# Cosformer attention and a gated FFN on one core: q and k of batch 4 loaded before batch 3's q is turned, and three tiles staged elsewhere

## The chip, the cores and the metric

One core of one Trainium2 chip runs the whole kernel. The time is device microseconds of one execution, as the median of some runs. One execution was also profiled; all times of single instructions come from that one.

## What is computed

```python
# q, k, v: (8 batches, 8 heads, 576 rows, 64); phi doubles 64 to 128 columns
phi(x) = concat(relu(x) * cos_row, relu(x) * sin_row)
kv  = phi(k)^T @ [v, 1]                        # per batch and head, 128 x 65
x   = (phi(q) @ kv)[:, :64] / (phi(q) @ kv)[:, 64]   # numerators / denominator
x   = x as (4608 tokens, 512)
out = (gelu(x @ w_gate) * (x @ w_val)) @ w_out        # 512 -> 1536 -> 512
```

Inputs and outputs are fp32 in HBM; the matmuls run in bf16.

## The kernel before, in words

The 4608 tokens are cut into eight batches of 576 for the attention and nine blocks of 512 for the FFN, so a batch's rows spill over block borders: block 2 takes the last 128 tokens of batch 1 and the first 384 of batch 2 (tiles t = 0, 1, 2 of 128 rows), block 3 takes t = 3 and 4 of batch 2 and the first 320 of batch 3. While TensorE (PE) works on the FFN of block n, the attention of batch n + 1 is made between its steps. The order of every engine's instructions is that of the Python text: nothing is reordered by a scheduler, and each engine runs its own list from front to back and waits where its next instruction must wait. SyncE (SP) is such a list too: it issues nearly all loads, stores and turns.

One batch goes through these stages:

- `load` (L95) brings q, k or v into a staging place. `stage` (L84) says which: st has three slots of 128 x 2304 fp32; sm and fs are two more places that later hold sums (sm the halves of hidden activations and partial products, L504; fs the differences of x).
- `prep` (L169) and `prep_both` (L183) scale: relu times sine on ACT, relu times cosine on ACT or DVE, into the tile phis. `prep_both` does q and k of a batch in one instruction of 128 x 512. `cast_v` (L207) casts half of v to bf16 (vx).
- `turn_q` (L220) writes qT, phi(q) transposed, by two DMA transposes. There is one qT; a new turn must wait until the numerators of the batch before have read it.
- `kv_unit` (L264) makes kv on PE in banks 6 and 7, ACT copies it.
- `nm_unit` (L309) makes the numerators of one tile t: 8 matmuls into two banks (6 and 7 unless told otherwise), then three DVE instructions (L322 to L324) that divide and leave x_sb. The next use of the banks waits for them.
- `turn_x` (L375) transposes x_sb by DMA into xT of the blocks concerned.

The FFN of a block has 12 steps jt, each 128 hidden columns: `gv_unit` (L420) makes 4 matmuls for gate and 4 for value, ACT the Gelu (L439), DVE the product (L442). It takes banks 0 and 1 or 2 and 3 in turn. In blocks 1 and 2 the first steps are cut into two halves of 256 tokens, because the later half of the block's x comes later: two units a step. `o_step` (L938) adds one or two of the seven half-size products that make the output matmul of the block before (L547, Strassen's scheme); sums come from DVE (L529), and ACT or DVE copies some partial products to sm (L565), in block 2 ACT. From block 3 on the gate and value matmuls use the same scheme (`group`, L650), with four differences of x made by POOL (`x_sum`, L630), and an ACT copy (L669) between the first two and the third of its products.

Around the change: `block1` (L975) is the FFN of block 1 with the attention of batch 2 and the scaling of q(3) and k(3) (batch in brackets); `block2` (L1025) is that of block 2 with the attention of batch 3 and the scaling of batch 4. Which loads SP issues at the end of which step stands in the table LOADS (L899), keyed by block and step; "0, 5" is the first five of nine row groups j of all heads, and a single 0 or 2 the first or second half of the heads. EARLY (L1015) says in which step of block 2 which row group of batch 4 is scaled, s for sine and c for cosine. SCALE (L964) does that for k(2), q(3) and k(3); keys from 12 on are steps of block 2.

SP's list between the turn of q(2) and block 3 is: turn q(2); load k(3); turn x(1,4); at steps 9 to 11 turn x(2,0), half of v(3), turn x(2,1), half of v(3), turn x(2,2); in block 2 turn q(3), turns x(2,3) and x(2,4), loads of batch 4 in six pieces, stores and the turns of x(3,t).

Of the kernel before, what the change touches and what calls it, by code (L numbers as in the profile page):

```python
# [16 lines left out]
def kernel(  # L17
# [13 lines left out]
    nc = tc.nc  # L31
# [8 lines left out]
    R = S // 64  # L40
# [25 lines left out]
    def bank(i):  # L66
        return ps[:, i]
# [13 lines left out]
    sm = sums.tile([128, NP * R * D], FP32)  # L81
    fs = fast.tile([128, 6 * BLK], FP32)

    def stage(name, b):  # L84
        early = {
            ("q", 1): 1, ("k", 1): sm, ("v", 1): fs, ("k", 2): 2, ("v", 2): 1,
            ("q", 3): fs, ("k", 3): 0, ("v", 3): 2,
            ("q", 5): 1, ("k", 5): 0, ("q", 7): 1, ("k", 7): 0,
        }
        at = early.get((name, b), "qkv".index(name))  # L90
        if isinstance(at, int):
            return st[:, at]
        return at[:, 0:NP * R * D].rearrange("p (m x) -> p m x", m=NP)
# [65 lines left out]
    act_copy, dve_copy = nc.scalar.copy, nc.vector.tensor_copy  # L159
# [5 lines left out]
    def phi_tile(name, b):  # L165
        phi[name, b] = phis[:, 1 if name == "k" else 2 * (b % 2) * (b > 2)]
        return phi[name, b]
# [15 lines left out]
    def prep_both(b, part, j, eng):  # L183
        for name in "qk":
            phi_tile(name, b)
        o = phis[:, b % 2:b % 2 + 2, :, j, part * D:(part + 1) * D]
        o = o.rearrange("p a m d -> p (a m) d")
        i = st[:, 0:2, :, j * D:(j + 1) * D].rearrange("p a m d -> p (a m) d")
        tab = (cos_t, sin_t)[part]
        if eng is nc.scalar:  # L190
            nc.scalar.activation(o, i, AF.Relu, scale=tab[:, j:j + 1])  # L191
        else:
            eng.tensor_scalar(o, i, 0.0, tab[:, j:j + 1], op0=ALU.max, op1=ALU.mult)
# [13 lines left out]
    def cast_v(b, m0, m1, copy, j0=0, j1=R):  # L207
        copy(  # L208
            vx[:, m0:m1, j0:j1, 0:D],
            staged["v", b][:, m0:m1, j0 * D:j1 * D].rearrange("p m (j d) -> p m j d", d=D),  # L210
        )
# [15 lines left out]
    def q_cols(b, t, h):  # L227
        c0 = min(t * 128, S - 128)
        return qT[b][:, h % 2, h // 2, c0:c0 + 128]
# [79 lines left out]
    def nm_unit(b, t, b0=6):  # L309
        for h in range(H):  # L310
            nc.tensor.matmul(  # L311
                bank(b0 + h // 4)[:, (h % 4) * (D + 1):(h % 4 + 1) * (D + 1)],
                lhsT=q_cols(b, t, h),
                rhs=kv_sb[b][:, h // 2, h % 2, :],
                start=True,
                stop=True,
            )
        nm = ps[:, b0:b0 + 2, 0:4 * (D + 1)].rearrange("p g (h d) -> p g h d", h=4)
        den = attn2.tile([128, 2, 4], FP32, name="den")
        rec = attn2.tile([128, 2, 4], FP32, name="rec")  # L320
        x = xsp.tile([128, 2, 4, D], BF16, name="x_sb")
        nc.vector.tensor_scalar_add(den, nm[:, :, :, D], EPS)  # L322
        nc.vector.reciprocal(rec, den)
        nc.vector.tensor_tensor(  # L324
            x,
            nm[:, :, :, 0:D],
            rec[:, :, :, None].to_broadcast([128, 2, 4, D]),
            op=ALU.mult,
        )
        xs[b, t] = x.rearrange("p g h d -> p (g h d)")  # L330
# [30 lines left out]
    def xT_block(blk):  # L361
        if blk not in xT:
            xT[blk] = xtp.tile([128, CT, BLK], BF16, name="xT")
        return xT[blk]

    def pieces(b, t):

        o = max(128 * (t + 1) - S, 0)
        c0, n = b * S + t * 128, 128 - o
        while n > 0:  # L370
            m = min(n, BLK - c0 % BLK)
            yield c0 // BLK, c0 % BLK, o, m
            c0, o, n = c0 + m, o + m, n - m

    def turn_x(b, t):  # L375
        x = xs.pop((b, t))
        for blk, c, o, m in pieces(b, t):
            nc.sync.dma_start_transpose(
                out=xT_block(blk)[:, :, c:c + m], in_=x[o:o + m, :]
            )  # L380

    def turn_x_pe(b, t, to, copy):
        x = xs.pop((b, t))
        p = bank16(to)[:, 0:CT * 128].rearrange("p (c n) -> p c n", c=CT)
        for ct in range(CT):
            nc.tensor.transpose(
                out=p[:, ct, :], in_=x[:, ct * 128:(ct + 1) * 128], identity=ident
            )
        for blk, c, o, m in pieces(b, t):
            copy(xT_block(blk)[:, :, c:c + m], p[:, :, o:o + m])  # L390
# [64 lines left out]
    def flush(engs=(nc.sync, nc.sync)):  # L455
        for i, o_sb in stores:
            store(engs, i, o_sb)
        stores.clear()
# [437 lines left out]
    def js(a, b):  # L896
        return tuple(range(a, b))

    LOADS = {  # L899
        (1, 2): [(3, "k")], (1, 9): [(3, "v", 0)], (1, 10): [(3, "v", 2)],  # L900
        (2, 2): [(4, "q", 0, 5), (4, "k", 0, 5), (4, "q", 5, R), (4, "k", 5, R), (4, "v")],
        (2, 9): [(5, "q", 0, 5), (5, "k", 0, 5)],
        (3, 1): [(5, "q", 5, R), (5, "k", 5, R), (5, "v")],
        (3, 9): [(6, "q", 0, 5), (6, "k", 0, 5)],
# [53 lines left out]
    def scale(b, name, sines_, cosines):  # L958
        for j in sines_:
            prep(name, b, 1, (j,), eng=nc.scalar)  # L960
        for j in cosines:
            prep(name, b, 0, (j,))
# [12 lines left out]
    def block1():  # L975
        b, n = 2, 1
        for jt in range(JT):
            i = jt - 9
            if i > 0:
                nm_unit(b, i, (6, 4, 6)[i])  # L980
                turn_x(b, i)
            if jt < 2:
                for i in range(2):
                    half, unit = divmod(2 * jt + i, 2)
                    x3 = lambda: turn_x_pe(1, 3, 5, dve_copy)
                    gv_unit(n, unit, half * HALF, HALF, between=x3 if jt == i == 0 else None)
                    j = JA + 2 * jt + i
                    prep("q", b, 1, (j,), eng=nc.scalar)
                    prep("q", b, 0, (j,))
            else:  # L990
                gv_unit(n, jt, between=(lambda: nm_unit(b, 0, 6)) if i == 0 else None)
            if i == 0:
                turn_x(b, 0)
            if jt % 3 == 1:
                flush()
            if jt == 2:
                prep("q", b, 0, (R - 1,))
                prep("q", b, 1, (R - 1,), eng=nc.scalar)
                turn_q(b)
                nm_unit(1, NT - 1)  # L1000
            if jt == 3:
                turn_x(1, NT - 1)
            if jt == 6:
                kv_unit(b)
            if jt in SCALE:
                scale(*SCALE[jt])
            if jt in (3, 4):
                cast_v(b, 2 * (jt - 3), 2 * (jt - 3) + 2, act_copy)
            if jt == 11:
                nm_unit(b, 3, 4)  # L1010
            start_loads(n, jt)
            if 4 <= jt < 8:
                wo_sum(("T3", "T1", "T2", "T4")[jt - 4])

    EARLY = {  # L1015
        5: "s0 c0", 6: "s1 c1 s2", 7: "c2 s3 c3", 8: "s4 c4", 9: "s5 c5", 10: "s6 c6",
        11: "s7 c7", 12: "s8 c8",
    }

    def early(jt):  # L1020
        for what in EARLY.get(jt, "").split():
            part = "cs".index(what[0])
            prep_both(4, part, int(what[1]), nc.scalar if part or jt > 7 else nc.vector)

    def block2():  # L1025
        b, n = 3, 2
        for jt in range(JT):
            if jt >= 4:
                gv_unit(n, jt, to=(2, 6) if jt == JT - 1 else None)
            else:  # L1030
                for i in range(2):
                    half, unit = divmod(2 * jt + i, 4)
                    gv_unit(n, unit, half * HALF, HALF)
                    if jt == i == 0:
                        nm_unit(2, 4)
                        turn_q(3)
            if 0 <= jt - 6 < NT:
                turn_x(b, jt - 6)
            if jt < JT - 1:
                o_step(n, jt)  # L1040
            if 0 <= jt - 5 < NT:
                nm_unit(b, jt - 5)
            if jt + JT in SCALE:
                scale(*SCALE[jt + JT])
            if jt < 2:
                cast_v(b, 2 * jt, 2 * jt + 2, act_copy)
            if jt == 3:
                kv_unit(b)
            early(jt)
            if jt == 1:  # L1050
                turn_x(2, 3)
                turn_x(2, 4)
            start_loads(n, jt)
            if jt in (8, 9):
                m = 2 * (jt - 8)
                cast_v(4, m, m + 2, (act_copy, dve_copy)[jt - 8])
            more(n, jt)

    turn[0] = 1
    block1()  # L1060
    block2()

    PREPS = {
# [124 lines left out]
```

## Time and profile before

| what | us |
|---|---|
| median of 3 runs | 313.39 (312.26 to 313.79) |
| the profiled execution | 313.79 |
| its span, first to last instruction | 311.4 |
| PE busy | 298.2 (96%) |
| DVE, ACT, POOL busy | 228.7, 201.4, 153.4 |
| PE clock, mean granted | 0.991 |

How to read it. The page cuts the span into 40 slices and gives each engine's busy share in tenths. A timeline row is: start, duration, engine, line of the kernel, operation, what it writes <- what it reads, shape, how many in a row, and in brackets how long the engine idled before it and what ended that. A q behind an engine's name is its issuing of DMAs. Of a DMA the profile also has the time from its issue to its landing. A wait list gives who waited, for whom, the total, how often and the longest.

In the profiled execution step 11 of block 1 ends on PE at 78.44 us, block 2 runs from 79.26 to 118.01 and block 3 begins there. The pieces of batch 4 that SP issued in block 2:

| load | issued at | us to landing |
|---|---|---|
| q, j 0 to 4 (640 KB) | 94.68 | 6.0 |
| k, j 0 to 4 (640 KB) | 95.31 | 7.0 |
| q, j 5 to 8 (512 KB) | 95.86 | 8.0 |
| k, j 5 to 8 (512 KB) | 96.35 | 9.0 |
| v, first half (576 KB) | 97.17 | 9.6 |
| v, second half (576 KB) | 97.98 | 10.3 |

### The profile page before, as it was taken

The page shows a single profiled execution, that of the slowest core. Times are in us where ns is not written, and L with a number is a line of the kernel's source. Part 1 is how long each engine was busy: PE and PEld are TensorE (multiplying, and loading weights), DVE is VectorE, ACT ScalarE, POOL GpSimd, SP SyncE. Part 2 cuts the span into 40 slices and gives each one's busy share as a digit, 9 for nine tenths or more (in the row PEclk, how much of TensorE's full clock was granted, in tenths as well). Part 3 has the DMA queues.
Part 4 walks back from the last instruction along what each step waited for, and adds up shares of the span by engine and source line. Part 5 has one row for each costly group of instructions (what it writes and reads, how often), then busy time and mean ns, then how long its engine had stood idle before and what let it go on. Part 6 is the DMA issues. An engine that isn't in the chain of part 4 may idle for free.

```text
span 311.4 us, 7900 instructions
## 1 busy us (share of the span) xinstructions
PE 298.2 (96%) x3071; PEld 225.9 (73%) x3071; DVE 228.7 (73%) x495; ACT 201.4 (65%) x394; POOL 153.4 (49%) x130
## 2 busy tenths in 40 slices
PE   8799999999899599999999999999999999999993
PEld 3574456655686267788878877878898888888882
DVE  5856996899973764788678867885779785866772
ACT  7864684997471578878587858785556465565530
POOL 6675430000000056737773777379965867297420
PEclk9999999999999989999999999999999999999998
DMA  7999999989997957996899699966652421213035
GB/s 277 246 178 239 319 308 396 301 119 217 199 157 233 293 122 204 124 353 129 222 121 360 129 216 122 344 103 108 93 107 40 93 42 37 45 24 69 1 78 126
DMA packets 73172, 53.66 MB, mean 172 GB/s; under 512 B 45392, under 2 KB 62544, under 8 KB 73136
## 3 DMA queue, kind: packets, MB, share of 16 engines
q1 hardware_dynamic: 63360, 41.17, 58.8%
q0 software_dynamic: 9696, 11.93, 16.7%
q8 instruction: 24, 0.39, 0.5%
q14 instruction: 12, 0.10, 0.1%
q10 hardware_dynamic: 80, 0.07, 0.1%
HBM read 37.75 MB, written 9.44 MB: 152 GB/s over the span
## 4 chain that ended last, share of the span: by engine, by line
PE 75%; DMA 7%; DVE 6%; issue 6%; ACT 3%; POOL 1%; SPq 1%; POOLq 0%; ACTq 0%; DVEq 0%
PE ps L650 29%; PE ps L547 19%; PE ps L430 17%; PE ps L463 3%; PE ps L311 3%; DMA st<-in_v_dram 2%; DMA st<-in_k_dram 2%; PE ps L270 2%; DMA wv_sb<-in_moe_w_val_dram 2%; DVE hT L442 2%; ACT phis L177 1%; DVE phis L179 1%; ACT vx L208 1%; POOL st L529 1%; ACT gel L439 1%
## 5 line engine op out<-in xcount | busy, mean ns | idle before, releaser
L630 POOL TENSOR_TENSOR fs<-xT 128x512 bf16<-128x512 bf16 x12 | 13.9, 1158 | 74.9 <-DVE den L322 66.8
L529 POOL TENSOR_TENSOR sm<-hT 128x768 bf16<-128x768 bf16 x24 | 39.4, 1641 | 20.1 <-PE ps L650 13.3
L430 PE MATMUL ps<-xT,wv_sb 128*128 128x512 bf16 (+1 forms) x208 | 49.1, 359 | 0.0
L430 PE MATMUL ps<-xT,wg_sb 128*128 128x512 bf16 (+1 forms) x208 | 48.3, 355 | 0.6 <-ACT phis L177 0.4
L442 DVE TENSOR_TENSOR hT<-gel,ps 128x512 bf16<-128x512 f32 (+1 forms) x52 | 32.1, 623 | 15.6 <-PE ps L430 11.2
L650 PE MATMUL ps<-fs,ws 128*128 128x256 bf16 x288 | 41.7, 273 | 0.0
L650 PEld LDWEIGHTS <-ws 128*128 128x128 bf16 x384 | 36.2, 98 | 4.6 <-ACT ps L669 0.3
L547 PEld LDWEIGHTS <-sm 128*128 128x128 bf16 x336 | 33.2, 99 | 6.5 <-issue 0.5
L439 ACT ACTIVATE gel<-ps 128x512 f32<-128x512 f32 (+1 forms) x52 | 28.3, 548 | 14.6 <-PE ps L430 13.4
L682 ACT ACTIVATE gel<-ps 128x512 f32<-128x512 f32 x30 | 17.9, 597 | 30.0 <-PE ps L650 30.0
L650 PE MATMUL ps<-xT,wg_sb 128*128 128x256 bf16 x240 | 36.0, 273 | 0.0
L690 DVE TENSOR_TENSOR ps<-fs,ps 128x512 f32<-128x512 f32 x30 | 20.9, 695 | 20.4 <-PE ps L650 14.2
L547 PEld LDWEIGHTS <-hT 128*128 128x128 bf16 x288 | 28.2, 98 | 6.2 <-issue 1.0
L430 PEld LDWEIGHTS <-wv_sb 128*128 128x128 bf16 x208 | 20.3, 98 | 17.0 <-issue 0.5
L560 DVE TENSOR_TENSOR o_sb<-sm,ps 128x256 f32<-128x256 f32 x56 | 23.4, 419 | 9.0 <-ACT sm L565 7.0
L191 ACT ACTIVATE phis<-st,sin_t 128x512 bf16<-128x512 f32 x36 | 25.7, 717 | 5.7 <-DMA st<-in_k_dram 5.7
L430 PEld LDWEIGHTS <-wg_sb 128*128 128x128 bf16 x208 | 19.3, 98 | 13.9 <-DMA xT<-x_sb 0.5
L529 POOL TENSOR_TENSOR sm<-hT,sm 128x768 bf16<-128x768 bf16 x12 | 19.7, 1642 | 15.7 <-PE ps L547 13.1
L324 DVE TENSOR_TENSOR x_sb<-ps,rec 128x512 bf16<-128x512 f32 x38 | 26.3, 691 | 1.3
L650 PEld LDWEIGHTS <-wg_sb 128*128 128x128 bf16 x240 | 23.1, 98 | 5.4
L177 ACT ACTIVATE phis<-st,sin_t 128x256 bf16<-128x256 f32 (+1 forms) x57 | 23.9, 480 | 1.5 <-DMA st<-in_k_dram 1.5
L547 PE MATMUL ps<-wo_sb,hT 128*128 128x256 bf16 x192 | 23.7, 272 | 0.9 <-DVE x_sb L324 0.9
(126 smaller groups left out, 590.5 us busy)
## 6 DMA issues: line engine op xcount, KB each, us to landing
out_dram<-o_sb SPq DMA_DIRECT2D x69, 128.0 KB, 3.0
st<-in_v_dram SPq DMA_DIRECT2D x12, 576.0 KB, 7.4
st<-in_q_dram SPq DMA_DIRECT2D x5, 640.0 KB, 5.0
st<-in_q_dram SPq DMA_DIRECT2D x5, 512.0 KB, 4.5
st<-in_k_dram SPq DMA_DIRECT2D x4, 640.0 KB, 6.0
st<-in_k_dram SPq DMA_DIRECT2D x4, 576.0 KB, 4.8
st<-in_q_dram POOLq DMA_DIRECT2D x4, 576.0 KB, 12.4
st<-in_k_dram SPq DMA_DIRECT2D x4, 512.0 KB, 5.3
```

The source lines that it names most:

```text
L177: nc.scalar.activation(o, i, AF.Relu, scale=tab[:, j:j + 1])
L191: nc.scalar.activation(o, i, AF.Relu, scale=tab[:, j:j + 1])
L324: nc.vector.tensor_tensor(x, nm[:, :, :, 0:D], rec[:, :, :, None].to_broadcast([128, 2, 4, D]), op=ALU.mult,)
L430: nc.tensor.matmul(bank(to[g])[:, 0:w], lhsT=wt[:, ct, js], rhs=xt[:, ct, c0:c0 + w], start=(ct == 0), stop=(ct == CT - 1),)
L439: nc.scalar.activation(gel[:, 0:w], bank(to[0])[:, 0:w], AF.Gelu)
L442: nc.vector.tensor_mul(hT[n][:, jt, c0:c0 + w], gel[:, 0:w], bank(to[1])[:, 0:w])
L529: eng.tensor_tensor(a[name][:, j0:j1], a[x][:, j0:j1], a[y][:, j0:j1], op=op)
L547: nc.tensor.matmul(at, lhsT=hs.setdefault(key, h_parts(n, p))[a][:, j], rhs=ts[b][:, j], start=(j == 0 and i in ((1, 2, 4, 5), (1, 4, 5))[ ...
L560: nc.vector.tensor_tensor(o, got[key, k], x, op=op)
L650: nc.tensor.matmul(to[:, 256 * half:256 * half + 256], lhsT=w_part(a, j * 128, (j + 1) * 128)[:, ct], rhs=xb[self.n][b][:, ct], start=(hal ...
L682: nc.scalar.activation(self.gel0, self.other, AF.Gelu)
L690: nc.vector.tensor_tensor(bank(val), self.m5, self.sum, op=ALU.add)
```

## The change

k(3) is staged in slot 2 instead of 0 and v(3) in sm instead of slot 2, which leaves slots 0 and 1 empty in block 1. k(3) and the first half of v(3) are loaded at step 4 of block 1 (k(3) stood at step 2, ahead of the turn of x(1,4)), the second half of v(3) at step 9, and the first halves of q(4) and k(4) at the end of step 11, ahead of the turn of q(3); they stood behind it. The numerators of batch 2's t = 3 go from step 11 of block 1 (banks 4 and 5) to behind the first unit of block 2 (banks 6 and 7), and those of t = 4 from there to behind the first unit of step 1, with the turn of q(3) behind them. The casts of v(3) come a step earlier, and so do those of v(4), which are now both on ACT. The scaling of batch 4 begins at step 4 and has one row group a step.

```diff
     early = {
         ("q", 1): 1, ("k", 1): sm, ("v", 1): fs, ("k", 2): 2, ("v", 2): 1,
-        ("q", 3): fs, ("k", 3): 0, ("v", 3): 2,
+        ("q", 3): fs, ("k", 3): 2, ("v", 3): sm,
...
     LOADS = {
-        (1, 2): [(3, "k")], (1, 9): [(3, "v", 0)], (1, 10): [(3, "v", 2)],
-        (2, 2): [(4, "q", 0, 5), (4, "k", 0, 5), (4, "q", 5, R), (4, "k", 5, R), (4, "v")],
+        (1, 4): [(3, "k"), (3, "v", 0)], (1, 9): [(3, "v", 2)],
+        (1, 11): [(4, "q", 0, 5), (4, "k", 0, 5)],
+        (2, 2): [(4, "q", 5, R), (4, "k", 5, R), (4, "v")],
...
             if jt == 11:
-                nm_unit(b, 3, 4)
+                cast_v(3, 0, 2, act_copy)
             start_loads(n, jt)
...
     EARLY = {
-        5: "s0 c0", 6: "s1 c1 s2", 7: "c2 s3 c3", 8: "s4 c4", 9: "s5 c5", 10: "s6 c6",
+        4: "s0 c0", 5: "s1 c1", 6: "s2 c2", 7: "s3 c3", 8: "s4 c4", 9: "s5 c5", 10: "s6 c6",
         11: "s7 c7", 12: "s8 c8",
     }
...
-            prep_both(4, part, int(what[1]), nc.scalar if part or jt > 7 else nc.vector)
+            prep_both(4, part, int(what[1]), nc.scalar if part or jt > 8 else nc.vector)
...
                     gv_unit(n, unit, half * HALF, HALF)
-                    if jt == i == 0:
-                        nm_unit(2, 4)
+                    if i == 0 and jt < 2:
+                        nm_unit(2, 3 + jt)
+                    if i == 0 and jt == 1:
                         turn_q(3)
             if 0 <= jt - 6 < NT:
                 turn_x(b, jt - 6)
+            if jt == 0:
+                cast_v(b, 2, 4, act_copy)
             if jt < JT - 1:
                 o_step(n, jt)
...
-            if jt < 2:
-                cast_v(b, 2 * jt, 2 * jt + 2, act_copy)
...
             start_loads(n, jt)
-            if jt in (8, 9):
-                m = 2 * (jt - 8)
-                cast_v(4, m, m + 2, (act_copy, dve_copy)[jt - 8])
+            if jt in (7, 8):
+                m = 2 * (jt - 7)
+                cast_v(4, m, m + 2, act_copy)
             more(n, jt)
```

## The prediction

> **What bounds the kernel now.** I read the page's slices first, then TensorE's waits between 80 and 180 us, then the timeline around the longest wait, then SyncE's own row of issues.
>
> ```profile
> PE   8799999999899599999999999999999999999993
> PEclk9999999999999989999999999999999999999998
> ```
>
> A slice is 7.8 us. PE is full except in the first slices, the 5 (101 to 109 us) and the end, so only time that PE loses counts. The 8 of PEclk stands just after the 5.
>
> ```profile
> PE ps L311 <- DVE x_sb L324: 3.1, 1, 3.1
> PE ps L547 <- DVE x_sb L324: 0.9, 1, 0.9
> ```
>
> These are nearly all of PE's waits in that window; both lie in block 2. The timeline shows what stands behind the long one:
>
> ```profile
> 95.31 0.45 SPq L98 DMA_DIRECT2D st<-in_k_dram  x1
> ...
> 102.44 0.72 ACT L191 ACTIVATE phis<-st,sin_t 128x512 bf16<-128x512 f32 x1 [5.67 <-DMA st<-in_k_dram]
> 102.46 0.49 DVE L193 TENSOR_SCALAR phis<-st,cos_t 128x512 bf16<-128x512 f32 x1 [3.29 <-DMA st<-in_k_dram]
> 103.07 0.58 ACT L439 ACTIVATE gel<-ps 128x512 f32<-128x512 f32 x1
> ...
> 103.68 0.69 DVE L442 TENSOR_TENSOR hT<-gel,ps 128x512 bf16<-128x512 f32 x1 [0.73 <-ACT gel L439]
> ...
> 105.98 0.69 DVE L324 TENSOR_TENSOR x_sb<-ps,rec 128x512 bf16<-128x512 f32 x1
> ...
> 106.72 0.42 PE L311 MATMUL ps<-kv_sb,qT 128*128 128x65 bf16 x8 [3.13 <-DVE x_sb L324]
> ```
>
> To be read upwards: PE waits for the evacuation of the numerators before (same two banks); that stands in DVE's queue behind a unit's product, which waits for ACT's Gelu; and both engines sat in front of batch 4's scaling until the first half of its k landed, 7.0 us after its issue. SyncE tells why that issue came at 95.31:
>
> ```profile
> 81.59 8.78 SPq L222 DMA_TRANSPOSE qT<-phis  x2
> 90.47 4.11 SPq L378 DMA_TRANSPOSE xT<-x_sb  x2
> 94.68 0.52 SPq L98 DMA_DIRECT2D st<-in_q_dram  x1
> ```
>
> The turn of batch 3's q and two turns of x hold SyncE for 13.1 us before the load.
>
> **Price of the long wait.** 3.13 us idle, and a slow clock after it: the windows view has 0.50 from 108 to 111 us. In the chain of waits the next eight matmuls of L430 take 2.56 us instead of 1.73, six of L547 1.28 instead of 0.66, eight of L311 0.44 instead of 0.26: 0.83 + 0.62 + 0.18 = 1.6. Together **4.7 us**. Behind it PE shows no wait over 0.2 us, so I let a gain here reach the end whole.
>
> **The loads ahead of the turn.** After the change SyncE reaches q and k of batch 4 behind the turn of x(2,2), which issues at 80.30 and takes 1.2: 81.5. Their slots are free (q of batch 2 scaled by 63 us, v of batch 2 cast by 67.5). With the 6.0 and 7.0 us to landing of today's issues they are there by about 89, and the first scaling comes at step 4, about 94.5. The wait is gone: **4.7 won**. Two 640 KB issues of 0.5 us each are only moved.
>
> **What is late next: the turn of q(3).** It rewrites qT, which the numerators of t=4 read, and these now stand behind unit 2 of step 1. I follow PE there. Its unit of step 11 ends at 78.44; the first unit of block 2 needs the turn of x(2,0). Today that issues at 75.72 and lands 3.4 later (79.1) behind both halves of k(3), issued at 70.45 and 71.84. Now the turn of x(1,4) goes first (1.2 us), k(3) at 71.65 (landing 5.0 later and 1.4 after that: 76.6, 78.0), half of v(3) behind it (1.45, as between the two halves of v(4): 79.5), and only then x(2,0). Bounds: 79.1 if half of v costs nothing, 80.5 if all is in turn; I take 79.8. PE: first unit 79.9, unit 0.87, numerators 0.26, unit 0.87: 81.9, where the pair of products starts; today 82.48, after the 0.86 us wait for banks 4 and 5, which goes because the numerators now use 6 and 7. Of those 0.6 us 0.26 is given back when t=4's numerators come; a 0.19 wait at 86.35 may go too. **0.4 won**, bounds -0.3 and 1.1.
>
> Then products 1.31, unit 0.87, numerators 0.26: the turn of q(3) issues at 84.4, not 81.59: 2.8 later. The two turns took 6.5 and 7.8 us to landing, 13.0 from the first issue to the second landing, with x(2,2) ahead of them until 86.1. Elsewhere (121.42 to 132.15) it is 10.7. So qT is complete between 95.1 and 97.4; its first reader, the numerators of t=0 at step 5, is at 97.50 today and at 97.1 then. Cost 0 to 0.3; I take 0.1.
>
> One page speaks against this order: the Trainium skill, "DMA: Bandwidth & Descriptors", section "Queues, rings and completion order", says that each DMA engine consumes a ring's descriptors in order. By it the 1.28 MB put ahead delay the turn; k's half would land near 87.5, and with the 8.6 us between the landings at 86.1 and 94.6 qT would be complete at 96.1, inside the range above.
>
> **v(4) on ACT.** The remaining four loads follow the turns. SyncE's way from turn to load was 13.1 us, with x turns of 2.0; with the 1.2 of the other x turns and 8.8 for the pair it is 11.2. So the first load goes at 95.6 to 97.5. A first load lands 4.5 (at 113.93) to 6.0 later (at 94.68), each further one 1.5 behind: half of v(4) is there 7.5 to 9.0 after the first issue, 103.1 to 106.5; middle 104.8. Today its cast runs at 112.53 at step 8; now at step 7, where ACT arrives at about 102.6. So ACT waits 0.5 to 3.9 us there, **a new wait**, and behind it stand the Gelu of step 8, the copies to sm, the scaling. How long may it? From the cast's start the next rows are spaced 1.04 (cast), 0.49 (Gelu), 0.25 (copy), 0.62 (sine), 0.61 (cosine). Up to block 3's first copy there are 2 casts, 4 Gelus, 2 copies, 4 sines, 3 cosines, and 0.58: 9.4 us. Without a stall PE needs that copy at 119.71 - 4.7 - 0.4 = 114.6, so the cast may start at 105.2. The numerators of t=4 of batch 3 (PE at 108.3) need the evacuation before them: cast and Gelu 1.65, unit's product 0.6, den to x_sb 1.1: 3.4 after the cast's start, so **104.9**. The middle value fits; the late end costs 1.6. I count 0.
>
> **The rest.** k(3) lands 1.1 later (78.0 for 76.9), but DVE first reads it at 78.62; ACT loses 1.1 there, where it idled 0.71 and 0.94 just after and DVE reached the unit's product only at 82.34. The casts of v(3) (1.14 each) move into ACT's 2.38 us of idle before 83.96; v's second half, issued at 77 without the wait for its slot, lands by 82 as before. Were that cover gone, ACT's copy to sm would slip by a cast, 1.1 us. One cast goes from DVE (0.85) to ACT; it is in the 9.4. The scaling of batch 4 begins a step earlier, 0.72 on ACT and 0.48 on DVE a step, where both idle over 1.2 us a step today (1.78 and 1.36 before step 5's Gelu and product). The subtractions on POOL (from 111.79) need the turn of x(3,2), which comes earlier with its evacuation; block 3 reads the first of four.
>
> **Sum.** 4.7 + 0.4 - 0.1 = 5.0. The profiled execution took 313.79 (span 311.4 and 2.4 around it), the slowest of three, 0.4 over their median 313.39. 313.79 - 5.0 = **308.8**; from the median it would be 308.4, and I keep the first.
>
> **Rivals.**
> 1. *The cast of v(4) is the new stall.* For it: the half lands at 106.5 at the late end, today it needs 9.6 us from its own issue, and it was moved a step earlier. Against: two loads fewer stand ahead. PE loses 1.6, up to 2.5 if the turn is late too: 310.4 to 311.3.
> 2. *Block 2 starts late.* If x(2,0) lands at 81 or later behind k and v of batch 3, PE idles 2.7 us instead of 1.4; 0.4 won becomes 0.9 lost: 310.1. Against: 1.7 MB were never that slow (1.45 us per 576 KB).
> 3. *Slower: the preload holds up the turn of q(3).* If its 3.2 us (two loads at 1.6) come on top of the slowest turn, qT is complete at 100.6, and PE waits 3.5 at t=0's numerators; after 3.1 the clock fell, so 1.6 more; the loads behind go at 100.7 and v comes at 109.7, 1.3 after the then allowed 108.4. 6.4 lost against 5.1 won: 315.1. It decides from a landing of qT of about 100. Against: the loads are issued 2.9 us before the turn, while PE still works towards it.
> 4. *The preload isn't early*, because SyncE waits at its slot or because scaling waits for the second halves: the 4.7 stay: 313.4.
>
> **Chances.** Forecast 0.52; rival 1 0.22; rival 2 0.09; rival 3 0.10; rival 4 0.07. The range takes the forecast, rivals 1 and 2: below it 0.7 more at the start of block 2 and 0.7 for the runs (half of their spread of 1.5), 307.4; above, rival 1's 311.3 and the same 0.7, 312.0. Some 2 in 10 are left out. What this measurement can tell from no change is about 0.5%, 1.6 us. Faster: 0.52 + 0.22 + 0.09 less 0.03 for their late ends, 0.80; same 0.03 + 0.07 + 0.01 of rival 3, 0.11; slower 0.09.
>
> **What would show it.** Right: no wait of PE over 1 us near 100 to 108, PEclk without the 8, ACT's first scaling of batch 4 with no DMA before it, one wait of ACT on v before 106, block 3's first matmul near 112.9 instead of 118.0, PE's first unit of block 2 near 79.9. Wrong: a wait of PE on qT near 97, on x_sb or ACT near 108 to 115, a second patch of clock 0.5, or x(2,0) landing past 80.5. The forecast falls if v's half lands past 107 or qT past 98.

## The result

The changed kernel takes 311.79 us as the median of 20 executions, beside 314.03 for the kernel before (20 executions): a ratio of 0.993, 95% interval 0.9903 to 0.9957. Measured again later it was 312.25 beside 313.66: 0.9966 (0.9943 to 0.9989). So the change is worth 1 to 2.2 us, not the 5.0 forecast; the time lies inside the range that was given, close to its upper end. Ratios and intervals leave out disturbed executions (one of k(3) first took 1752 us, three of no preload 313.8 to 347) and medians don't; in the group of the fill and the three kernels with k(3) first that took out a third of those of the kernel before, so that their ratios stand 0.2 to 0.3% high against the medians.

The page of the profiled execution (312.38 us, span 310.6): its rows PE and PEclk.

```profile
span 310.6 us, 7905 instructions
...
PE   8799999999799999999999999999999999999993
...
PEclk9799999999899999999999999999999999999998
```

The 5 at 101 to 109 us is gone, and so is the 8 of PEclk after it. In their place stand a 7 and an 8 at 78 to 85 us, where the kernel before had nines: a wait and a slow clock at the start of block 2. (The 7 of PEclk near 11 us is another fall of the clock, at the start of this execution, ahead of everything that was changed; the profiled execution of the kernel before had none there.) PE's waits between 60 and 130 us:

```profile
PE ps L430 <- DMA xT<-x_sb: 2.3, 1, 2.3
PE ps L311 <- DVE x_sb L324: 0.8, 2, 0.5
```

Before, the first line of such a list was 3.1 us for x_sb. Now PE waits for a turned x. SyncE's own list ahead of that wait, from the timeline (start, duration):

```profile
70.90 1.73 SPq L378 DMA_TRANSPOSE xT<-x_sb  x1
72.81 0.95 SPq L98 DMA_DIRECT2D st<-in_k_dram  x2
73.82 0.46 SPq L98 DMA_DIRECT2D sm<-in_v_dram  x1
76.31 1.19 SPq L378 DMA_TRANSPOSE xT<-x_sb  x1
```

ACT and PE in the same stretch of the timeline:

```profile
79.44 0.91 ACT L177 ACTIVATE phis<-st,sin_t 128x256 bf16<-128x256 f32 x2 [2.46 <-DMA st<-in_k_dram]
...
81.52 0.60 PE L430 MATMUL ps<-xT,wg_sb 128*128 128x256 bf16 x4 [2.32 <-DMA xT<-x_sb]
```

The turn of x(2,0) is issued at 76.31, as soon as its x is made, and lands 5.1 us later, behind k(3) and half of v(3). The issue lists of the DMA view give its time to landing, before:

```profile
xT<-x_sb SPq DMA_TRANSPOSE x1, 3.4
```

and in the changed kernel:

```profile
xT<-x_sb SPq DMA_TRANSPOSE x1, 5.1
```

PE has nothing to do from 79.20 to 81.52. Then the windows view, whose column after the engines is the granted clock:

```profile
83.00:86.00 3.00, 3.00 (x16) 2.13 (x15) 1.80 (x5) 1.43 (x2) 0.00 (x0) 0.50 0.88 239
```

Half speed for three microseconds and more after a wait of 2.3. Later in the block, ACT and PE:

```profile
108.96 1.16 ACT L208 CAST vx<-st 128x1152 bf16<-128x1152 f32 x1 [3.04 <-DMA st<-in_v_dram]
...
110.64 0.69 DVE L442 TENSOR_TENSOR hT<-gel,ps 128x512 bf16<-128x512 f32 x1 [1.82 <-ACT gel L439]
...
111.68 0.69 DVE L324 TENSOR_TENSOR x_sb<-ps,rec 128x512 bf16<-128x512 f32 x1
...
112.42 0.42 PE L311 MATMUL ps<-kv_sb,qT 128*128 128x65 bf16 x8 [0.54 <-DVE x_sb L324]
```

ACT stands 3.04 us before the cast of v(4), and the chain of Gelu, product and evacuation behind it reaches PE as 0.54.

To compare executions with different starts, two stretches of PE's row serve below: from the first matmul of kv(2) in block 1 (L270, at 67.76 before and 68.35 after) to the first of kv(3) in block 2, and from there to block 3's first matmul (L650). They hold the same matmuls in every kernel but for the idle ones of the fill. Each row is one profiled execution.

| kernel | kv(2) to kv(3) | kv(3) to block 3 | sum |
|---|---|---|---|
| before | 23.7 | 26.6 | 50.3 |
| changed | 25.7 | 22.7 | 48.4 |
| places only | 26.2 | 22.2 | 48.4 |
| numerators only | 23.5 | 28.7 | 52.2 |
| v(3) behind | 24.4 | 22.0 | 46.4 |
| v(3) early | 24.4 | 22.3 | 46.8 |
| fill | 24.7 | 22.3 | 46.9 |
| changed, again | 25.9 | 22.0 | 47.9 |
| fill, again | 24.3 | 22.2 | 46.5 |
| k(3) first | 22.6 | 22.6 | 45.2 |
| k(3) first, casts late | 23.1 | 22.8 | 45.9 |
| k(3) first, v(4) first | 22.6 | 22.0 | 44.6 |
| no preload | 23.4 | 24.3 | 47.6 |
| numerators back | 23.4 | 22.0 | 45.4 |

In the changed kernel the second stretch gives 3.8 us (4.5 in its second profile) and the first takes 2.0 back (2.2).

### The profile page after: what moved, and what is told of

It reads as the page before. It is cut to its first block, busy times and chain, and to the rows that moved or that the text cites. A ratio compares the mean times of both kernels' runs of the same rounds, so it can differ in the third digit from the quotient of the medians.

```text
span 310.6 us, 7905 instructions
## 1 busy us (share of the span) xinstructions
PE 298.2 (96%) x3071; PEld 226.9 (73%) x3071; DVE 228.1 (73%) x495; ACT 202.2 (65%) x394; POOL 153.4 (49%) x130
## 4 chain that ended last, share of the span: by engine, by line
PE 78%; DMA 6%; issue 5%; DVE 4%; ACT 2%; SPq 2%; POOL 1%; POOLq 0%; DVEq 0%; ACTq 0%
PE ps L650 29%; PE ps L547 19%; PE ps L430 18%; DMA st<-in_v_dram 5%; PE ps L463 3%; PE ps L311 3%; PE ps L270 2%; DMA xT<-x_sb 2%; PE ps L233 1%; SPq L98 1%; DVE hT L442 1%; ACT phis L177 1%; PE ps L401 1%; ACT gel L439 1%; PE ps L386 1%
## 5 line engine op out<-in xcount | busy, mean ns | idle before, releaser
L650 PE MATMUL ps<-fs,ws 128*128 128x256 bf16 x288 | 41.7, 273 | 0.0
L650 PEld LDWEIGHTS <-ws 128*128 128x128 bf16 x384 | 36.2, 98 | 4.6 <-ACT ps L669 0.3
L439 ACT ACTIVATE gel<-ps 128x512 f32<-128x512 f32 (+1 forms) x52 | 28.5, 548 | 13.7 <-PE ps L430 12.3
L650 PE MATMUL ps<-xT,wg_sb 128*128 128x256 bf16 x240 | 36.0, 273 | 0.0
L547 PEld LDWEIGHTS <-hT 128*128 128x128 bf16 x288 | 28.7, 100 | 5.7
L560 DVE TENSOR_TENSOR o_sb<-sm,ps 128x256 f32<-128x256 f32 x56 | 23.4, 419 | 12.0 <-ACT sm L565 10.0
L650 PEld LDWEIGHTS <-wg_sb 128*128 128x128 bf16 x240 | 23.1, 98 | 5.4
L547 PE MATMUL ps<-wo_sb,hT 128*128 128x256 bf16 x192 | 24.7, 279 | 0.0
```

Source lines behind the costliest of these rows:

```text
L439: nc.scalar.activation(gel[:, 0:w], bank(to[0])[:, 0:w], AF.Gelu)
L547: nc.tensor.matmul(at, lhsT=hs.setdefault(key, h_parts(n, p))[a][:, j], rhs=ts[b][:, j], start=(j == 0 and i in ((1, 2, 4, 5), (1, 4, 5))[ ...
L560: nc.vector.tensor_tensor(o, got[key, k], x, op=op)
L650: nc.tensor.matmul(to[:, 256 * half:256 * half + 256], lhsT=w_part(a, j * 128, (j + 1) * 128)[:, ct], rhs=xb[self.n][b][:, ct], start=(hal ...
```

## The experiments

The theory after the result: the missing gain is lost at the start of block 2, where the turn of x(2,0) lands late behind the loads that were put ahead of it, and the idling costs clock as well. The rival: it is lost later, at v(4) and the turn of q(3).

**One part alone: the places.** The kernel before with k(3) and v(3) staged, loaded and cast as in the change; batch 4's loads, its scaling and the numerators as before.

```diff
-            ("q", 3): fs, ("k", 3): 0, ("v", 3): 2,
+            ("q", 3): fs, ("k", 3): 2, ("v", 3): sm,
...
-        (1, 2): [(3, "k")], (1, 9): [(3, "v", 0)], (1, 10): [(3, "v", 2)],
+        (1, 4): [(3, "k"), (3, "v", 0)], (1, 9): [(3, "v", 2)],
...
```

> The kernel before with only the new places and load times of k(3) and v(3) and the earlier casts of v(3); no preload of batch 4, numerators as before. Theory (the missing gain is lost at the start of block 2, where the turn of x(2,0) lands behind k(3) and half of v(3)): PE waits about 2 us at its first unit of block 2 instead of 0.4, with or without a fall of the clock, and the long stall at batch 4's scaling stays: ratio to before 1.004 to 1.012. Rival (the places cost nothing, the gain is lost later, at qT and v(4)): x(2,0) lands as before and the ratio is 0.998 to 1.002.

Measured: 312.35 beside 313.26, 0.9952 (0.9921 to 0.9984): a little faster, which neither expected (the interval just reaches the rival's 0.998). PE's waits in it:

```profile
PE ps L430 <- DMA xT<-x_sb: 2.9, 1, 2.9
PE ps L311 <- DVE x_sb L324: 0.4, 1, 0.4
```

And its timeline at the scaling of batch 4:

```profile
96.21 0.45 SPq L98 DMA_DIRECT2D st<-in_k_dram  x1
...
101.83 0.72 ACT L191 ACTIVATE phis<-st,sin_t 128x512 bf16<-128x512 f32 x1 [2.90 <-DMA st<-in_k_dram]
...
106.11 0.42 PE L311 MATMUL ps<-kv_sb,qT 128*128 128x65 bf16 x8 [0.37 <-DVE x_sb L324]
```

The wait of 2 us and more at block 2's start came as the theory said. But the long stall went, without any preload: k(4) is issued at 96.21 and lands at 101.72; counted from kv(2) that is 34.3 us, beside 34.6 before, so hardly earlier, and ACT still waits for it. PE simply comes 2.5 us later to the place where it used to wait. When k(4) lands is set by SyncE's list, not by PE, so the two waits do not add: the earlier one takes the place of the later. With 2.5 lost in the first stretch and 4.3 won in the second (the wait and the slow clock after it), this part alone was worth, by its profile, as much as the whole change (both sums are 48.4).

**The other part alone: the numerators,** and the turn of q(3) behind them.

```diff
-            if jt == 11:
-                nm_unit(b, 3, 4)
...
-                    if jt == i == 0:
-                        nm_unit(2, 4)
+                    if i == 0 and jt < 2:
+                        nm_unit(2, 3 + jt)
+                    if i == 0 and jt == 1:
                         turn_q(3)
```

> The kernel before with only the numerators of batch 2's t = 3 and 4 moved into block 2's first units and the turn of q(3) behind them. Theory: the 0.86 us wait for banks 4 and 5 goes, but the turn issues some 2 us later and with it, behind it in SyncE's list, q and k of batch 4, so the long stall grows by about as much: net 0.5 to 1.5 slower, ratio 1.001 to 1.005. Rival (the turn has slack, the moved numerators are a clean gain): the long stall stays at 3.1 and the ratio is 0.997.

Measured: 316.08 beside 313.26, 1.0081 (1.0051 to 1.0111). The mechanism is the theory's, its size larger. PE's longest wait:

```profile
PE ps L311 <- DVE x_sb L324: 5.4, 1, 5.4
```

SyncE's list in the same kernel, the turn of q(3) first:

```profile
85.46 8.92 SPq L222 DMA_TRANSPOSE qT<-phis  x2
94.47 2.51 SPq L378 DMA_TRANSPOSE xT<-x_sb  x2
97.07 0.53 SPq L98 DMA_DIRECT2D st<-in_q_dram  x1
```

The turn goes 2.8 us later (counted from kv(2)), the loads of batch 4 stand behind it, and the stall grows from 3.1 to 5.4. The wait for banks 4 and 5 is gone, as expected. So this part is a loss alone and needs the preload.

**v(3) out of the way.** The changed kernel with both halves of v(3) behind the turn of x(2,0):

```diff
-        (1, 4): [(3, "k"), (3, "v", 0)], (1, 9): [(3, "v", 2)],
+        (1, 4): [(3, "k")], (1, 9): [(3, "v")],
```

> The changed kernel with both halves of v(3) loaded at step 9 behind the turn of x(2,0); k(3) at step 4 as changed. Theory: x(2,0) lands 1.4 earlier, PE's wait at block 2's start falls from 2.3 to about 0.9 and the clock falls there less often: 1.4 to 3 us under the changed kernel, ratio to before 0.983 to 0.989. ACT may wait up to 1 us for v. Rival (k(3)'s late landing, through ACT's Gelu and DVE's product of step 11, holds PE anyway): the wait moves to the second unit and the ratio stays at 0.993.

Measured: 311.10 beside 313.26, 0.9888 (0.9843 to 0.9933). PE's wait for x(2,0) is 1.0 instead of 2.3, and the clock holds in the profile; 0.35 and 0.44 come back as waits for ACT and DVE. The ratio is at the upper end of what the theory said, and its interval just reaches the rival's 0.993; the trace decides for the theory, for no wait near 2 us moved to the second unit.

The changed kernel with v(3) loaded by POOL's queue behind block 0, where sm has been free since k(1) was scaled:

```diff
     for m in (0, 2):
         load(nc.sync, "q", 3, m, m + 2)
+    for m in (0, 2):
+        load(nc.gpsimd, "v", 3, m, m + 2)
...
-        (1, 4): [(3, "k"), (3, "v", 0)], (1, 9): [(3, "v", 2)],
+        (1, 4): [(3, "k")],
```

> The changed kernel with v(3) loaded some 20 us earlier by POOL's queue, behind block 0, into the same place sm. Theory: as the run with v behind, without ACT's wait: x(2,0) behind k(3) alone, wait at block 2's start about 0.9, ratio 0.982 to 0.988; what the early v costs in front (q(3) and the turn of q(2) up to 1 us later) lies beside PE's work. Rival (k(3) decides): 0.993.

Measured: 310.26 beside 313.26, 0.9882 (0.9845 to 0.9918). The time is the theory's, but half of its mechanism isn't: in this profile x(2,0) landed at 80.68, 4.8 us after its issue, with no v(3) ahead, and PE waited 2.0. The second half of k(3) landed only 3.0 us after the first. So k(3) itself, issued behind the turn of x(1,4), was still too late (its second half landed 12.3 us after kv(2), 11.0 in the changed kernel, partly because it was also issued 0.6 later); the rest of the gain in this profile is the clock, which did not fall.

**k(3) first.** As v(3) early, with the turn of x(1,4) moved behind the loads of k(3):

```diff
-            if jt == 3:
-                turn_x(1, NT - 1)
...
             start_loads(n, jt)
+            if jt == 4:
+                turn_x(1, NT - 1)
```

> As the run with v(3) loaded early by POOL, and k(3) issued at step 4 ahead of the turn of x(1,4) instead of behind it. Theory: k(3) and with it x(2,0) land 1.5 earlier, PE's wait at block 2's start falls to 0.5 or less: ratio 0.982 to 0.985. Rival (with block 2's start earlier the next bound takes it back: the cast of v(4) on ACT or the turn of q(3)): waits of PE on qT near 97 or on x_sb near 108 grow to 1 to 2 us and the ratio stays at 0.987 to 0.989.

Measured: 309.16 beside 313.09; 0.9894 (0.9835 to 0.9953). PE's waits:

```profile
PE ps L311 <- DVE x_sb L324: 0.9, 3, 0.4
PE ps L430 <- DMA xT<-x_sb: 0.5, 1, 0.5
```

The ratio by itself is the rival's figure, and its interval covers the theory's too; the trace decides. Nothing over 0.5 us is left, x(2,0) landed 1.6 us earlier than with v(3) early (11.2 from kv(2), not 12.7), and the first stretch is 22.6, 3.1 shorter than in the changed kernel, the clock's share included. What the rival foresaw, 1 to 2 us at qT or at v(4), did not come, although ACT waited 2.9 us for v(4).

Two variants of it. The casts of v(4) back at steps 8 and 9:

```diff
-            if jt in (7, 8):
-                m = 2 * (jt - 7)
+            if jt in (8, 9):
+                m = 2 * (jt - 8)
```

> As the run with k(3) first, with v(4)'s two casts back at steps 8 and 9 (both on ACT). If v(4)'s landing holds ACT at step 7 and through it PE, this gains 0.5 to 1.5 over that run; if it does not, the two agree within 0.3.

Measured: 309.03 beside 313.09, 0.9899 (0.9851 to 0.9948): not told apart from k(3) first. PE's wait for x(2,0) was 1.4 in its profile, the one of 0.4 at the evacuation was replaced by 0.6 for a Gelu. Moving the casts back gains nothing.

v(4) loaded ahead of the second halves of q(4) and k(4):

```diff
-        (2, 2): [(4, "q", 5, R), (4, "k", 5, R), (4, "v")],
+        (2, 2): [(4, "v"), (4, "q", 5, R), (4, "k", 5, R)],
```

> As the run with k(3) first, with v(4) loaded ahead of the second halves of q(4) and k(4) in block 2. v(4)'s first half lands 3 us earlier, so ACT's wait at step 7 falls from some 3 us to under 1; the second halves land near 107, before step 9 reads them. If v(4) holds PE: 0.5 to 1.5 faster than the run with k(3) first; if not, within 0.3.

Measured: 307.91 beside 313.09, 0.9867 (0.9818 to 0.9917), the best of all. ACT no longer waits before the cast (103.14), and PE's list is down to

```profile
PE ps L430 <- ACT phis L177: 0.6, 1, 0.6
PE ps L311 <- DVE x_sb L324: 0.3, 1, 0.3
```

The first line is the unit at 80.29; x(2,0) landed at 80.2. It is 0.8 us faster than k(3) first by the ratios and 0.5 by the stretches, but the intervals overlap: that v(4) held PE by about half a microsecond is likely and not shown.

**The clock.** The changed kernel with ten idle matmuls where PE waits:

```diff
+                    if jt == i == 0:
+                        dummies(10, 4)
                     gv_unit(n, unit, half * HALF, HALF)
```

> The changed kernel with ten idle matmuls (128x512, about 2.2 us, into bank 4, read by nobody) ahead of block 2's first unit, where PE waits 2.3 us for x(2,0). Theory: the idling there also costs clock (0.5 for 3.4 us after it); filled, the clock holds, and the kernel gains 1 to 1.7 us: ratio to before 0.988 to 0.990, no fall of the clock near 82. Rival (the fall has another cause, or the idling is all of the loss): 0.993 or more.

Measured: 310.43 beside 313.09, 0.994 (0.9909 to 0.9971). The clock held in the profile, and the ratio was the rival's, but the changed kernel had been measured at another time. So both were run again side by side.

> The changed kernel once more, as the partner of the fill on the same chip: 0.993 of before.

> The changed kernel with the ten idle matmuls ahead of block 2, beside the changed kernel itself. If the clock falls in most executions because PE idles 2.3 us there: 1 to 1.6 us faster than its partner. If the fall is rare or costs little: within 0.5 of it.

Measured: the changed kernel 312.25, 0.9966 (0.9943 to 0.9989); filled 310.46, 0.9895 (0.9867 to 0.9923). The two intervals don't meet: the fill is 1.8 us faster, and each of its six executions was faster than each of the other twelve. The windows view, from 80 to 84 us, of the changed kernel in this group:

```profile
80.00:84.00 4.00, 2.40 (x18) 1.86 (x19) 2.68 (x9) 3.05 (x7) 0.00 (x0) 0.60 0.87 222
```

The same of the filled one:

```profile
80.00:84.00 4.00, 3.55 (x34) 2.51 (x33) 3.11 (x11) 3.66 (x9) 0.00 (x0) 1.00 0.93 222
```

The matmuls compute nothing that is used; they only keep PE busy through what was a 2.9 us wait in that execution. The clock is 0.60 on the mean without them and 1.00 with them. Over the executions the mean clock was 0.984 to 0.992 in eleven of the twelve without them (the twelfth, 0.994, is the profiled one, which had the fall) and 0.994 to 0.998 with them. In the first measurement 4 of the 20 executions of the changed kernel had 0.996 or more, too high for a fall of this length anywhere in the kernel (half of 3.41 us is 0.0055 of 310); they took 309.3 to 310.9 us, about as long as the filled kernel. So the fall comes in most executions, not in all.

Why not in all can be read from the profiles. In all 14 of them the clock changes on a grid of 3.41 us: the two falls of the changed kernel begin at 11.04 and 82.72, 21 steps apart. What goes with a fall is how long PE idles within one step, not how long the wait is. The windows view of such steps, the changed kernel first (the column after the window's length is PE's busy time):

```profile
79.31:82.72 3.41, 1.20 (x17) 1.14 (x18) 2.70 (x8) 3.27 (x7) 0.00 (x0) 1.00 1.13 234
82.72:86.14 3.42, 3.42 (x20) 2.44 (x17) 1.81 (x5) 1.66 (x3) 0.00 (x0) 0.50 0.92 248
```

The same with v(3) early, where a step ended within the wait of 2.0:

```profile
77.14:80.55 3.41, 1.59 (x7) 0.56 (x6) 1.89 (x6) 0.22 (x1) 0.00 (x0) 1.00 1.09 160
80.55:83.97 3.42, 2.96 (x32) 2.56 (x33) 2.60 (x9) 3.42 (x8) 0.00 (x0) 1.00 0.20 38
```

PE was idle for 2.2 us of the first step, and the next ran at half clock; in the other kernel it was idle for 1.8, and the clock held. From the clock's first record on, 4 to 7 us after the start, every step with 2.0 us or more of idling was followed, in the 14 profiles, by one at half clock, and none with 1.8 or less; of three with 1.9 one was.

**No preload, start repaired.** The kernel with the places only, and v(3) early and k(3) first in it; batch 4 as before the change.

```diff
+    for m in (0, 2):
+        load(nc.gpsimd, "v", 3, m, m + 2)
...
-        (1, 4): [(3, "k"), (3, "v", 0)], (1, 9): [(3, "v", 2)],
+        (1, 4): [(3, "k")],
...
-            if jt == 3:
-                turn_x(1, NT - 1)
...
+            if jt == 4:
+                turn_x(1, NT - 1)
```

> Start of block 2 repaired (v(3) early by POOL, k(3) ahead of the turn of x(1,4)), but no preload: batch 4's six loads behind the turn of q(3), scaling, casts of v(4) and numerators at the steps of the kernel before. Theory (the two losses lie side by side: PE is late either at block 2's start or at batch 4's scaling, and the later of the two counts): with the start repaired PE runs into the long stall of 3 us again and the time is that of before, ratio 0.995 to 1.002, 3 us and more over the best run. Rival (the early k and v are the whole gain and the preload is idle): no stall at the scaling, ratio 0.985 to 0.990.

Measured: 311.25 beside 313.66, 0.9893 (0.9862 to 0.9924). The time is the rival's, the trace shows the theory's stall. PE's waits:

```profile
PE ps L311 <- DVE x_sb L324: 2.4, 1, 2.4
PE ps L547 <- DVE x_sb L324: 0.8, 1, 0.8
```

And ACT's first scaling of batch 4 on the timeline:

```profile
100.65 0.72 ACT L191 ACTIVATE phis<-st,sin_t 128x512 bf16<-128x512 f32 x1 [4.93 <-DMA st<-in_k_dram]
```

With PE early again, the wait at batch 4's scaling is back, but only 2.4 long and with no fall of the clock behind it (the second stretch is 24.3, not 26.6; 1.6 of this is the clock). Counted from kv(2), the loads of batch 4 issue 0.9 earlier and k(4) lands 1.1 earlier, though the turn of q(3) issues where it did before; that v(3) is gone from SyncE's list and from the queue is the likely reason, and no run shows it alone. The wait's 2.4 us fell into two steps of the clock's grid, 1.8 of it into the first. So both sides were partly wrong: k(3) and v(3) loaded this way are a gain of their own of some 2.5 us, and the stall which the preload is to remove is still there without it.

**What the preload and the moved numerators are worth then.** The best kernel with the numerators and the turn of q(3) where they stood before:

```diff
             if jt == 11:
+                nm_unit(b, 3, 4)
...
-                    if i == 0 and jt < 2:
-                        nm_unit(2, 3 + jt)
-                    if i == 0 and jt == 1:
+                    if jt == i == 0:
+                        nm_unit(2, 4)
                         turn_q(3)
```

> The best kernel so far (v(3) early, k(3) first, v(4) ahead of the second halves) with batch 2's numerators t = 3 and 4 and the turn of q(3) where they stood before the change. If moving them was a gain of its own: the 0.86 us wait for banks 4 and 5 is back, 0.5 to 0.9 slower than the best. If the earlier turn of q(3) outweighs it: v(4) and all loads 2.5 us earlier, no slower than the best or up to 0.5 faster.

Measured: 309.58 beside 313.66, 0.9868 (0.984 to 0.9896). PE's longest wait:

```profile
PE ps L547 <- DVE x_sb L324: 0.9, 1, 0.9
```

The wait for banks 4 and 5 is back, and the first stretch is 0.8 longer than in the best kernel; the second is the same, so the earlier turn buys nothing once the loads stand ahead of it. Against the kernel without preload, on the same chip, it is 2.2 us faster by the stretches, 1.7 by the medians and 0.8 by the ratios, whose intervals overlap: that is the preload, with the earlier scaling and casts and with v(4) first. Its size is not settled; that the stall is gone, the trace shows.

## Why the prediction was wrong

**The price of the long wait** held in the profile: the second stretch without a stall is 22.0 in the runs and was 26.6 before, 4.6 for the 4.7 forecast. Not every execution pays it whole: of the 23 of the kernel before in the last group 4 had a mean clock of 0.996 or more, and so no fall. The step that let this gain "reach the end whole" did not fail: from block 3's first matmul to the end it is 193.4 us before and 193.8 in the changed kernel.

**The step that failed is the one that placed the turn of x(2,0)** at 79.8 and PE's first unit at 79.9, and won 0.4 there. Counted from kv(2), x(2,0) landed 13.0 later, where 12.0 had been forecast (11.4 before; the forecast's late bound of 80.5 is 12.7), and PE waited 2.3, not 1.4. k(3)'s second half was 0.8 later than forecast. Most of that, 0.6, lies in its issue: the step reckoned 1.2 us of SyncE for the turn of x(1,4) ahead of it, and it held SyncE for 1.9 (from 70.90 to 72.81 in the list above). From the first half's issue to the second half's landing the step was nearly right, 6.35 reckoned and 6.55 measured. Behind it, half of v(3) took its full 1.5 us (landing at 80.88), where the step had counted half of that. Both causes were tried: with v(3) behind, x(2,0) landed 1.3 us earlier, and k(3) ahead of the turn of x(1,4) made it land 1.6 earlier than v(3) early alone. Rival 2 named this place and this cause, with 2.7 us of idling, and gave it 0.09. Its condition of 81 is 13.2 from kv(2), and 13.0 was measured.

**What no step had priced: the clock at that place.** The forecast reckoned 1.6 us for a slow clock only after a wait of over 3.1 us, the one that its trace showed, and rival 2 had none. The fall came after 2.3, in most executions, and the side-by-side runs put the fill of that wait at 1.8 us. The page "TensorE: Matmul & The Clock Gate" of the Trainium skill, section "What's actually happening", has a window of 3.4 us that runs freely and does not begin with the kernel; the grid of 3.41 us in the profiles agrees, and so does the length of a stretch of 0.5 here (82.7 to 86.1). Waits of 2.3, 2.9, 3.1 and 5.4 us were followed by a fall, waits of 2.0 and 2.4 (v(3) early, no preload), which put 1.8 us of idling into one step, were not.

Together: first stretch 0.4 won forecast, 2.0 lost. Of the difference of 2.4, 1.0 is lateness and 1.4 is left for the clock; the two fills shorten this stretch by 1.0 and 1.6.

**The wait of ACT for v(4)** came (3.04 us) and reached PE as 0.54, in place of 0. In the changed kernel's second profile ACT waited 2.28 and PE not at all. Counted from kv(2), the turn of q(3) issued 2.9 later than forecast, because PE was late, and v(4)'s first half landed some 3.5 later than the middle value. Since PE was late too, the bound of 104.9 for the cast moved along, and the cost stayed small: right in mechanism, mis-sized by up to 0.5, and partly by luck, for two errors met. The forecast of the cast's slack is borne out by k(3) first: a wait of 2.9 cost PE under 0.4.

**The turn of q(3)**: no wait of PE on qT, as forecast (0.1). With the preload issued 4.7 us ahead, the pair took 10.8 us from issue to second landing, the forecast's lower end of 10.7. Issued right behind the loads (numerators back), it took 12.3.

**The wait for banks 4 and 5**: gone, and worth 0.8 by the run with the numerators back, as forecast.

**The rivals.** Rival 1 (the cast of v(4)) came in part: its wait of 0.5 to 3.9 on ACT, but 0 to 0.54 on PE instead of 1.6. Rival 2 all but came, and its price of 0.9 lost was 2.0, most of the rest being the clock, which it left out. Rival 3 (slower) did not come: nothing waited for qT. Rival 4 did not come. Not foreseen by any: that the start of block 2 and the scaling of batch 4 are two waits of which the later one counts, so that the places alone, which make PE late at the first, take away the second.

## What to carry to other kernels

When a load is moved ahead in a queue, the transfer whose landing starts the next stage has to be followed through that queue like a wait on the critical engine; here 1.0 us there was worth 2.4, the clock included. When the issue of a transfer does not depend on the engine that waits for it, the wait grows if that engine is made early and disappears if the engine is late: price such waits by when the transfer lands, not by how long the wait is. And a wait of TensorE of some 2 us, as here, is to be priced with a fall of the clock behind it that comes in a part of the executions; a run that fills the wait shows what it is worth.

## What the runs showed of the hardware that was not expected

- The granted clock fell to 0.5 for 3.41 us after waits of TensorE of 2.3 and 2.9 us; ten idle matmuls in such a wait gave 1.8 us back (312.25 to 310.46).
- It changed on a grid of 3.41 us whose place against the kernel differs from execution to execution (in the two profiles of the changed kernel the fall began 14.4 and 13.0 us after kv(2)). Every step with 2.0 us or more of idling of PE was followed by one at half clock, and none with 1.8 or less. So a wait of 2.4 us that lay across two steps (no preload) cost no clock, and one of 2.3 that lay mostly in one (the changed kernel) did.
- The turn of x(1,4) held SyncE for 1.7 to 2.1 us where it was issued directly behind the turn of q(2), and for 1.2 to 1.3 where k(3)'s loads stood between them.
- The two halves of k(3), 576 KB each, landed 2.7 to 3.0 us apart in the five kernels in which they were issued behind the turn of x(1,4) (changed, places only, v(3) behind, v(3) early, fill), and 1.4 to 1.5 apart in six of the seven in which they were issued ahead of it (2.7 in the seventh, casts late). That is less of a difference than it seems: in the five they were issued 0.5 us apart, not 1.0 to 1.5, and the first one landed sooner (3.9 to 4.3 us after its issue, not 4.6 to 5.1). From the first issue to the second landing it was 6.5 to 7.2 us, and 6.1 to 6.5 in the six (7.8 in the seventh). What the rest comes from is open; no run was made for it.
